# Fetching q, k and v of three batches head by head through GpSimd's queue, with a register for the head and a cast in flight

## The chip, the cores and the metric

The kernel runs on one core of a Trainium2 chip. The metric is the time of one run in device microseconds (us). The kernel before takes 238.6 us as the median of its runs (238.37 to 239.58). Every kernel that is compared below was run on one chip beside the kernel before, in the same rounds. A run in which the time lies over 1.5% above the fastest of its kernel is put down as slow. Ratios leave such runs out; the medians quoted are of all runs, and e10, e12 and e13 each have one slow run among them. The experiments ran in sets on different chips, on which the kernel before took 238.6 to 240.0 us, so kernels of different sets are compared best by their ratios.

The engines carry these names in the profile: PE is TensorE (matmuls), PEld its weight loads, DVE VectorE, ACT ScalarE, POOL GpSimd, SP SyncE, which here only issues DMA transfers.

## The reference

Attention with two kinds of heads is followed by a small feed-forward layer. Shapes: batch 4, 8 heads, sequence 768, head size 64; then 3,072 tokens of width 512 through a hidden layer of 2,048.

```python
scores = scale * np.matmul(q, k.transpose(0, 1, 3, 2))
causal = rel >= 0                                   # rel = query position - key position
stream_keep = causal & (is_sink | in_win)           # the first 4 keys, or the last 64
mask = np.where(retr[0, :, 0, 0, None, None], full_mask, stream_mask)   # by head
a = softmax of np.where(mask, scores, -1e9)
attn = np.matmul(a, v)
x = attn.transpose(0, 2, 1, 3).reshape(B * S, H * D)
h = x @ w_in
return (h - np.tanh(h)) @ w_out
```

Which heads see all earlier keys ("retrieval" heads) and which see only a window is known from the input `is_retrieval` at run time alone.

## The kernel before

The 3,072 tokens are worked in 12 tiles of 256 (three tiles a batch). The first batch (tiles 0 to 2) treats all heads alike and masks them. For batches 1 to 3 (tiles 3 to 11) the heads are put in the order of a rank, retrieval heads first, so that window heads can skip most scores. The rank is computed on the chip, and eight registers of GpSimd hold which head has which rank.

The program is made by a small planner. Every instruction is handed to it with an estimated duration in ns, its reads and writes and, for a transfer, its packets. It simulates the engines and writes each engine's instructions down in the order in which they ran in that simulation. Each engine then runs in that order on the chip.

```python
def op(self, eng, ns, fn, r=(), w=(), dma=None, prio=None, port=False, after=None, behind=None):
    ...   # dependencies from the keys in r and w; dma = (packets, ns of one packet)
```

For tiles 3 to 11 SP fetches fp32 q, k and v, each as two loads of 128 rows x 8 heads (1,024 packets of 256 bytes), and GpSimd casts to fp16, one rank at a time, the register choosing the head:

```python
op(
    "SP", max(420, 128 * nh * 1.1),
    lambda ...: nc.sync.dma_start(
        out=raw_of(nm, t)[:, i, h0 : h0 + nh, :],
        in_=src[b, h0 : h0 + nh, s0 : s0 + 128, :].rearrange("h p d -> p h d"),
    ), ..., dma=(128 * nh, 18.3), after=after,
)
...
def cast_ranked(t):
    for half in range(2):
        for nm in ("qk", "v"):
            for rank in range(half * HH, half * HH + HH):
                def fn(nm=nm, rank=rank):
                    at = bass.ds(regs["POOL"][rank], 1)
                    ...   # v in the same way
                    nc.gpsimd.tensor_copy(
                        out=t16[t % 2][:, :, :, rank : rank + 1, :],
                        in_=raws["rqk", t][0]()[:, :, :, at, :],
                    )
                op("POOL", 300 if nm == "v" else 430, fn, ...)
    for i in range(NB):          # two transposes by DMA on SP's queue, when all of q and k are cast
        nc.sync.dma_start_transpose(out=qk[b % 2][:, :, g * NB + i, 0:128], in_=t16[t % 2][:, i]...)
    ...
```

The transposed `qk` is what the score matmuls on TensorE read. So a tile goes: load, cast, transpose, scores. Tiles 1 and 2 already come by GpSimd's own queue with a cast in flight (`load_cast`, 1,024 packets an issue, no register), and so do the weights of the hidden and output layers.

The softmax here doesn't subtract the row's maximum and nothing guards it: scores larger than these inputs give would overflow.

Of the kernel before, what the change touches and what calls it, by code (L numbers as in the profile page):

```python
# [7 lines left out]
FP32 = mybir.dt.float32  # L8
# [8 lines left out]
class Plan:  # L17
# [16 lines left out]
    def op(self, eng, ns, fn, r=(), w=(), dma=None, prio=None, port=False, after=None, behind=None):  # L34
        i = len(self.ops)
        deps = set() if after is None else {after}
        for k in r:
            if k in self.writer:
                deps.add(self.writer[k])
            if k[0] in self.PSUM:  # L40
                deps.update(j for j in self.readers.get(k, ()) if self.ops[j][0] != eng)
            self.readers.setdefault(k, []).append(i)
# [16 lines left out]
    def run(self):  # L59
# [45 lines left out]
        while len(order) < n:  # L105
# [28 lines left out]
            _, ns, _, _, dma, _, port, _ = self.ops[i]  # L134
            self.start[i] = t
# [4 lines left out]
            for u in followers[i]:  # L140
                ready[u] = max(ready[u], t + ns)
                left[u] -= 1
                if not left[u]:
                    enqueue(u)
            if dma:
                packets, each = dma
                rings["POOL" if e == "POOL" else "SP"].append(
                    [i, t + ns + (1200 if e == "POOL" else 300), each, packets * each / 16]
                )
            else:  # L150
                finish(i, t + ns + self.RESULT[e])
# [6 lines left out]
def kernel(  # L158
# [35 lines left out]
    RAW, PT, XB, GB, XTB, THB, OB = 2, 3, 3, 3, 3, 3, 3  # L194
# [28 lines left out]
    gate = const.tile([1, 1], FP16, name="gate")  # L223
# [33 lines left out]
    def program(first):  # L257
# [30 lines left out]
        def paired(nm, t):  # L288

            return nm != "v" and t == 0  # L290

        def load(t, names="qkv", halves=(None,), blocks=range(NB), after=None):

            b, g = divmod(t, NG)
            for half in halves:
                h0, nh = (0, H) if half is None else (half * HH, HH)
                for nm in names:
                    src = {"q": q, "k": k, "v": v}[nm]
                    tag = "rv" if nm == "v" else "rqk"
                    if (tag, t) not in raws:  # L300
                        idx = rot[tag] = rot.get(tag, -1) + 1
                        shape = [128, NB, H, D] if nm == "v" else [128, NB, 2, H, D]
                        raws[tag, t] = (
                            lazy(raw_pool, shape, FP32, tag, f"raw_{tag}{t}"), idx
                        )
                    if paired(nm, t):
                        op(
                            "SP", max(420, 128 * nh * 1.1),
                            lambda nm=nm, src=src, h0=h0, nh=nh: nc.sync.dma_start(
                                out=raw_pairs(nm, t)[:, h0 : h0 + nh, :, :].rearrange(  # L310
                                    "p h e d -> p h (e d)"
                                ),
                                in_=src[b, h0 : h0 + nh, g * TT : (g + 1) * TT, :].rearrange(
                                    "h (p e) d -> p h (e d)", e=NB
                                ),
                            ),
                            w=[
                                key for x in (range(2) if half is None else (half,))
                                for key in raw_keys(nm, t, x)
                            ],  # L320
                            dma=(128 * nh, 26.0), after=after,
                        )
                        continue
                    for i in blocks:
                        s0 = g * TT + i * 128
                        op(
                            "SP", max(420, 128 * nh * 1.1),
                            lambda nm=nm, i=i, src=src, s0=s0, h0=h0, nh=nh: nc.sync.dma_start(
                                out=raw_of(nm, t)[:, i, h0 : h0 + nh, :],
                                in_=src[b, h0 : h0 + nh, s0 : s0 + 128, :].rearrange("h p d -> p h d"),  # L330
                            ),
                            w=[
                                key for x in (range(2) if half is None else (half,))
                                for key in raw_keys(nm, t, x, (i,))
                            ],
                            dma=(128 * nh, 18.3), after=after,
                        )
# [13 lines left out]
        def raw_keys(nm, t, half, blocks=range(NB)):  # L351
            tag = "rv" if nm == "v" else "rqk"
            return [(tag, raws[tag, t][1], nm, half, i) for i in blocks]
# [11 lines left out]
        def load_cast(t, w_after=(), names="qkv"):  # L365

            b, g = divmod(t, NG)
            for nm in names:
# [13 lines left out]
                if nm == "v":  # L382
                    for i in range(NB):
# [3 lines left out]
                            dma=(128 * H, 18.5),  # L387
                        )
                    continue
                for i in range(NB):  # L390
                    behind(
                        930, lambda fn=fn, i=i: fn((i,)), r=w_after,
                        w=[key for half in range(2) for key in t16_keys(nm, t, half, (i,))],
                        dma=(128 * H, 18.5),
# [37 lines left out]
        for half in range(2):  # L432
            load(0, "qk", (half,))
            load(0, "v", (half,))
# [102 lines left out]
        def by_rank(after):  # L537

            def dve(ns, fn, r, w):
                op("DVE", ns, fn, r=r, w=w, after=after)  # L540
# [82 lines left out]
                r=["A4", "A40", "A41", "A43"], w=["mS"], port=True, after=after,  # L623
# [4 lines left out]
                r=["mS3"], w=["mS"], port=True, after=after,  # L628
            )
            for e, et in (("POOL", Engine.Pool), ("DVE", Engine.DVE)):  # L630
# [7 lines left out]
                op(e, 900, get, r=["perm"], w=["regs" + e])  # L638
# [9 lines left out]
        def t16_keys(nm, t, half, blocks=range(NB)):  # L648
            return [("t16", t % 2, nm, half, i) for i in blocks]

        def cast_qk(t, engines, halves=range(2)):

            for half in halves:
                for nm, es in zip("qk", engines):
                    hs = slice(half * HH, half * HH + HH)
                    cast_op(
                        es[half], NB * HH * D,
                        lambda nm=nm, hs=hs: t16[t % 2][:, :, "qk".index(nm), hs, :],
                        lambda nm=nm, hs=hs: raw_of(nm, t)[:, :, hs, :],
                        r=raw_keys(nm, t, half), w=t16_keys(nm, t, half),  # L660
                    )

        def cast_ranked(t):
# [4 lines left out]
            for half in range(2):  # L668
                for nm in ("qk", "v"):
                    for rank in range(half * HH, half * HH + HH):  # L670

                        def fn(nm=nm, rank=rank):
                            at = bass.ds(regs["POOL"][rank], 1)
                            if nm == "v":
                                nc.gpsimd.tensor_copy(  # L675
                                    out=v1s[b]()[:, lo : lo + NB, rank : rank + 1, 0:D],
                                    in_=raw_of("v", t)[:, :, at, :],
                                )
                            else:
                                nc.gpsimd.tensor_copy(  # L680
                                    out=t16[t % 2][:, :, :, rank : rank + 1, :],
                                    in_=raws["rqk", t][0]()[:, :, :, at, :],
                                )

                        op(
                            "POOL", 300 if nm == "v" else 430, fn,
                            r=["regsPOOL"] + [
                                key for x in range(2) for n_ in nm for key in raw_keys(n_, t, x)
                            ],
                            w=[("v1", b, g, half)] if nm == "v" else [  # L690
                                key for n_ in nm for key in t16_keys(n_, t, half)
                            ],
                            port=True,
                        )
            for i in range(NB):

                def turn(i=i):
# [7 lines left out]
                    r=[key for half in range(2) for n_ in "qk" for key in t16_keys(n_, t, half)],  # L705
# [83 lines left out]
        def cast_v(t, engines=("POOL", "POOL"), halves=range(2)):  # L789
# [5 lines left out]
            for half in halves:  # L795
# [4 lines left out]
                    r=raw_keys("v", t, half), w=[("v1", b, g, half)],  # L800
# [27 lines left out]
        def st_T(n, eq="DVE", ek="DVE"):  # L828
            t, hp = divmod(n, HP)
            b, g = divmod(t, NG)  # L830
            for x, (nm, e) in enumerate((("q", eq), ("k", ek))):
# [9 lines left out]
                def turn(x=x, tp=tp):  # L841
# [7 lines left out]
                    "PE", 112, turn, r=t16_keys(nm, t, hp * 2 // HP) + ["ident"], w=[key],  # L849
# [412 lines left out]
        cast_qk(0, (("ACT", "ACT"), ("ACT", "DVE")), (0,))  # L1262
        load_cast(1, [("rv", 0, "v", 0, 1)], "qk")
# [10 lines left out]
        cast_v(0, ("POOL", "POOL"), (0,))  # L1274
        cast_qk(0, (("ACT", "ACT"), ("ACT", "DVE")), (1,))
# [8 lines left out]
        cast_v(0, ("POOL", "POOL"), (1,))  # L1284
# [16 lines left out]
        else:  # L1301
            load(2)
            scale_v(0, "POOL")
        scale_v(1)
        if first:

            def wait_tile_2():
                nc.sync.dma_start(out=gate[:], in_=t16[0][0:1, 0, 1, 0, 0:1])

# [133 lines left out]
```

## Time and profile before

| | before |
|---|---|
| median time | 238.6 us |
| profiled span | 236.7 us |
| TensorE busy | 221.5 us (94%) |
| GpSimd busy | 90.5 us (38%) |
| packets of SP's queue / of GpSimd's | 92,642 / 15,168 |
| granted TensorE clock, mean | 1.000 |

Two lines of the page show the row of 40 slices of the span (5.9 us each; a digit is the busy share in tenths) for GpSimd, and the clock that TensorE was granted.

```profile
POOL 5999420089818068480814904606300000000000
PEclk9999999999999999999999999999999999999999
```

GpSimd has whole slices with nothing to do, even between 40 and 160 us where it handles tiles 3 to 11, and the clock is full throughout. This is the timeline of GpSimd for part of a tile (start, length, then what ran; in brackets idle time before it and what ended it).

```profile
69.86 2.58 POOL L680 CAST t<-raw_rqk 128x256 f16 x6 [5.52 <-DMA raw_rqk<-in_k_dram]
...
74.51 2.13 POOL L675 CAST v<-raw_rv 128x128 f16 x6
```

Six casts of q and k take 2.58 us.

### The profile page before, as it was taken

How to read it: one execution, taken by the hardware profiler on the slowest of the kernel's cores; microseconds unless marked ns; L12 is line 12 of the kernel's file. 1: busy time of each engine (PE TensorE's matmuls, PEld its weight loads, DVE VectorE, ACT ScalarE, POOL GpSimd, SP SyncE). 2: the span in 40 equal slices, each digit the busy share in tenths (PEclk: the TensorE clock that was granted, in tenths of full speed). 3: DMA queues.
4: the chain of work that ended last, by engine and by line, in shares of the span. 5: the costliest groups of instructions: out<-in, count | busy, mean ns of one | idle time of the engine just before them, and what ended most of it. 6: DMA issues, size and time to landing. Idle time of an engine off the chain costs nothing. (4 is left out here: it accounts for less than half of the span.)

```text
span 236.7 us, 5895 instructions
## 1 busy us (share of the span) xinstructions
PE 221.5 (94%) x2220; PEld 157.8 (67%) x2220; DVE 139.0 (59%) x343; ACT 143.6 (61%) x221; POOL 90.5 (38%) x218
## 2 busy tenths in 40 slices
PE   0889899999999999999999999999999999999991
PEld 0346687756776777777676777776776777777661
DVE  1856665864488657767666655667766546443300
ACT  3668677884588387466686649537759464444320
POOL 5999420089818068480814904606300000000000
PEclk9999999999999999999999999999999999999999
DMA  5999999999997999979989695998712101310121
GB/s 128 209 140 172 204 181 204 197 228 224 206 225 182 151 248 184 227 153 206 239 168 214 136 186 130 186 171 179 134 47 66 38 31 47 90 38 9 44 89 51
DMA packets 108130, 35.29 MB, mean 149 GB/s; under 512 B 100290, under 2 KB 104642, under 8 KB 108098
## 3 DMA queue, kind: packets, MB, share of 16 engines
q1 hardware_dynamic: 92642, 28.98, 60.5%
q0 software_dynamic: 15168, 5.77, 20.7%
q8 instruction: 18, 0.29, 0.5%
q10 hardware_dynamic: 288, 0.14, 0.2%
q14 instruction: 14, 0.11, 0.2%
HBM read 27.27 MB, written 6.29 MB: 142 GB/s over the span
## 5 line engine op out<-in xcount | busy, mean ns | idle before, releaser
L1135 PE MATMUL ph<-xT,win 128*128 128x256 f16 x768 | 101.7, 273 | 0.6 <-DMA win<-in_moe_w_in_dram 0.3
L1194 PE MATMUL po<-wout,gt 128*128 128x512 f16 (+1 forms) x400 | 98.0, 371 | 0.3 <-ACT ot L1170 0.3
L1148 ACT ACTIVATE th<-ph 128x512 f32<-128x512 f32 x96 | 57.6, 601 | 59.6 <-PE ph L1135 58.2
L1155 DVE SCALAR_TENSOR_TENSOR gt<-th,ph 128x512 f16<-128x512 f32 x96 | 65.4, 684 | 44.9 <-ACT th L1148 44.4
L1135 PEld LDWEIGHTS <-win 128*128 128x128 f16 x768 | 80.0, 114 | 13.0 <-issue 1.9
L961 ACT ACTIVATE pt<-sc 128x1024 f16<-128x1024 f32 (+1 forms) x78 | 68.5, 926 | 11.4 <-PE sc L941 10.9
L1194 PEld LDWEIGHTS <-gt 128*128 128x128 f16 x400 | 36.4, 98 | 24.6 <-issue 0.9
L680 POOL CAST t<-raw_rqk 128x256 f16 x72 | 28.5, 440 | 63.3 <-DMA raw_rqk<-in_k_dram 48.1
L1030 PEld LDWEIGHTS <-pt 128*128 128x128 f16 x552 | 25.9, 98 | 10.4 <-issue 0.9
L1030 PE MATMUL av<-v,pt 128*128 128x65 f16 x304 | 26.0, 195 | 0.1
L941 PE MATMUL sc<-qk 64*128 64x128 f16 (+1 forms) x412 | 23.8, 240 | 1.7 <-DVE qk L826 1.7
L941 PEld LDWEIGHTS <-qk 64*128 64x128 f16 x412 | 13.7, 94 | 13.5 <-issue 8.9
L675 POOL CAST v<-raw_rv 128x128 f16 x72 | 21.1, 335 | 4.2 <-DMA raw_rv<-in_v_dram 4.2
L1060 DVE TENSOR_TENSOR x16t<-av,rinv 128x128 f32 x72 | 20.8, 289 | 2.3 <-DVE rinv L1050 0.3
L1030 PE MATMUL av<-vf,pt 128*128 128x65 f16 x248 | 19.6, 193 | 0.0
L1170 ACT ACTIVATE ot<-po 128x512 f32<-128x512 f32 (+1 forms) x24 | 14.3, 596 | 8.5 <-PE po L1194 8.4
L996 DVE TENSOR_TENSOR pt<-pt,m 128x1024 f16<-128x1024 f16 x16 | 12.3, 768 | 8.0 <-ACT pt L961 8.0
L1050 DVE RECIPROCAL rinv<-av 128x4 f32<-128x4 f32 x48 | 8.6, 179 | 13.4 <-PE av L1030 13.4
L986 DVE TENSOR_TENSOR pt<-pt,mS 128x512 f16<-128x512 f16 x24 | 9.8, 449 | 6.7 <-ACT pt L961 6.7
L843 PEld LDWEIGHTS <-t 128*128 128x128 f16 x48 | 3.9, 107 | 8.9 <-ACT t L644 6.8
L523 DVE TENSOR_SCALAR m<-A,thr 128x512 f16<-128x512 f16 x16 | 7.4, 501 | 1.7 <-PE sc L928 1.2
L751 POOL TENSOR_TENSOR vf<-v,rflagr 128x260 f16<-128x260 f16 x12 | 7.5, 634 | 0.0
(95 smaller groups left out, 90.8 us busy)
## 6 DMA issues: line engine op xcount, KB each, us to landing
out_dram<-ot SPq DMA_DIRECT2D x23, 256.0 KB, 2.3
raw_rqk<-in_q_dram SPq DMA_DIRECT2D x20, 256.0 KB, 4.7
raw_rqk<-in_k_dram SPq DMA_DIRECT2D x20, 256.0 KB, 4.5
raw_rv<-in_v_dram SPq DMA_DIRECT2D x18, 256.0 KB, 4.4
win<-in_moe_w_in_dram POOLq DMA_DIRECT2D x4, 512.0 KB, 8.8
wout<-in_moe_w_out_dram POOLq DMA_DIRECT2D x4, 512.0 KB, 12.4
raw_rv<-in_v_dram SPq DMA_DIRECT2D x4, 128.0 KB, 4.7
t<-in_q_dram POOLq DMA_DIRECT2D x4, 128.0 KB, 9.5
```

Source lines behind the costliest of these rows:

```text
L675: nc.gpsimd.tensor_copy(out=v1s[b]()[:, lo : lo + NB, rank : rank + 1, 0:D], in_=raw_of("v", t)[:, :, at, :],)
L680: nc.gpsimd.tensor_copy(out=t16[t % 2][:, :, :, rank : rank + 1, :], in_=raws["rqk", t][0]()[:, :, :, at, :],)
L941: nc.tensor.matmul(out=sc()[:, hh, o : o + nb * 128].rearrange("p (i c) -> p i c", c=128), lhsT=ks.rearrange("p i c -> p (i c)")[p_, jb * ...
L961: lambda pt=pt, gi=gi, wid=wid, sc=sc: nc.scalar.activation(out=pt()[:, :, 512 * gi : 512 * gi + wid], in_=sc()[:, :, 0:wid], func=AF.Exp, ...
L996: nc.vector.tensor_mul(out=pv, in0=pv, in1=m4[:, h0 : h0 + 2, 256:512].unsqueeze(2).to_broadcast([128, 2, 2, 256]),)
L1030: nc.tensor.matmul(out=av()[:, i, hh, :], lhsT=pt()[:, hh, co : co + 128], rhs=vv, start=(jb == first_jb), stop=(jb == qb),)
L1060: nc.vector.tensor_mul(out=x16s[t]()[:, :, at, :], in0=av()[:, :, hh : hh + 1, 0:D], in1=rinv()[:, :, hh : hh + 1].unsqueeze(3).to_broadca ...
L1135: nc.tensor.matmul(out=ph()[:, j, :], lhsT=w()[:, cb, c0 + fb % 4 : c0 + 512 : 4], rhs=xTs[t]()[:, cb, :], start=(cb == 0), stop=(cb == HP ...
L1148: lambda: nc.scalar.activation(out=th()[:], in_=ph()[:], func=AF.Tanh, scale=1.0 / XS),
L1155: lambda: nc.vector.scalar_tensor_tensor(out=gts[t]()[:, u * FU : (u + 1) * FU, :], in0=th()[:], scalar=-XS, in1=ph()[:], op0=ALU.mult, op ...
L1170: nc.scalar.activation(out=ot()[:, c0:c1], in_=po()[:, c0:c1], func=AF.Copy, scale=1.0 / XS)
L1194: nc.tensor.matmul(out=po()[:, c0:c1], lhsT=gts[t]()[:, f, ts * 128 : ts * 128 + 128], rhs=w_out_t[f // 4]()[:, f % 4, c0:c1], start=(f == ...
```

## The change

The intent is to have no fp32 copies and no casts for batches 1 to 3. GpSimd fetches each head's 256 rows straight to its rank's place, the head's number taken from the register, and the DMA casts on the way.

```diff
-    RAW, PT, XB, GB, XTB, THB, OB = 2, 3, 3, 3, 3, 3, 3
+    RAW, PT, XB, GB, XTB, THB, OB = 1, 4, 3, 3, 3, 3, 3
...
-        def cast_ranked(t):
+        def load_ranked(t, names):
...
+            for nm in names:
+                for rank in range(H):
+                    def fn(nm=nm, src=src, rank=rank):
+                        at = bass.ds(regs["POOL"][rank], 1)
+                        o = (
+                            v1s[b]()[:, lo : lo + NB, rank, 0:D] if nm == "v"
+                            else t16[t % 2][:, :, "qk".index(nm), rank, :]
                         )
+                        nc.gpsimd.dma_start(
+                            out=o,
+                            in_=src[b, at, g * TT : (g + 1) * TT, :].rearrange(
+                                "h (i p) d -> p i (h d)", p=128
+                            ),
+                        )
+                    behind(
+                        380, fn, r=["regsPOOL"], ...
+                        dma=(NB * 128, 14.0), after=PACE.get((t, nm)),
+                    )
...
+        def turn_ranked(t):        # the two transposes, as before
...
-        for half in range(2):
-            load(0, "qk", (half,))
-            load(0, "v", (half,))
+        for names, pairs in [("qk", (0,)), ("qk", (1,)), ("v", (0, 1)), ("qk", (2, 3)), ("v", (2, 3))]:
+            load(0, names, pairs)
```

Each of the nine tiles thus has 24 issues of 256 packets (3 tensors x 8 heads) in place of 6 issues by SP and 16 casts. Besides, q and k of tile 0 come by pairs of heads, the rank computation comes a tile earlier, one more buffer holds softmax results (`PT`), and some of the planner's constants change.

## The prediction

> **What bounds the kernel now.** I read the page's busy table and its row of slices, then stretches of the span with each engine's busy time, then TensorE's waits, then the queues, the groups and single transfers.
>
> ```profile
> PE 221.5 (94%) x2220; PEld 157.8 (67%) x2220; DVE 139.0 (59%) x343; ACT 143.6 (61%) x221; POOL 90.5 (38%) x218
> PE   0889899999999999999999999999999999999991
> ```
> TensorE (PE) is busy for 221.5 of 236.7 us, so all that a change can win without less matmul work is the other 15.2 us. The stretches (columns: length, then busy us of PE, weight loads, VectorE, ScalarE, GpSimd) say where these lie.
>
> ```profile
> 0.00:14.00 14.00, 7.12 (x46) 3.17 (x46) 7.08 (x21) 7.34 (x12) 10.86 (x26) 1.00 1.18 156
> 14.00:40.00 26.00, 23.48 (x276) 17.88 (x273) 16.35 (x41) 19.13 (x34) 13.75 (x17) 1.00 1.46 186
> 40.00:80.00 40.00, 39.05 (x446) 27.35 (x445) 26.83 (x82) 27.51 (x41) 22.31 (x59) 1.00 1.04 207
> 80.00:220.00 140.00, 140.00 (x1381) 101.53 (x1380) 86.06 (x196) 86.21 (x130) 43.60 (x117) 1.00 0.68 137
> 220.00:236.70 16.70, 11.81 (x81) 7.86 (x79) 2.63 (x5) 3.37 (x6) 0.00 (x0) 1.00 0.15 52
> ```
> Idle TensorE: 6.9 us before 14, 2.5 from 14 to 40, 1.0 from 40 to 80, **nothing from 80 to 220**, 4.9 in the tail. A busy TensorE need not be a full one, so I counted the stretch from 200 to 220 us: 93 matmuls of 256 columns and 46 of 512, at the 0.107 and 0.213 us that back-to-back starts in the timeline show, make 9.9 + 9.8 = 19.7 of 20 us. It is full. The granted clock is 1.00 throughout. The longest TensorE waits are the first one and very little else:
>
> ```profile
> PE tp0q L843 <- ACT t L644: 6.0, 1, 6.0
> PE sc L941 <- DVE qk L826: 1.7, 3, 0.7
> PE tp0k L843 <- ACT t L644: 0.5, 1, 0.5
> ```
> The casts that the change removes, GpSimd's two big groups, do wait for transfers, but nobody on TensorE waits long for them (one 0.4 us wait of a weight load). So they are off the path.
>
> ```profile
> L680 POOL CAST t<-raw_rqk 128x256 f16 x72 | 28.5, 440 | 63.3 <-DMA raw_rqk<-in_k_dram 48.1
> L675 POOL CAST v<-raw_rv 128x128 f16 x72 | 21.1, 335 | 4.2 <-DMA raw_rv<-in_v_dram 4.2
> ```
>
> **What the Trainium skill says.** "DMA: Bandwidth & Descriptors", section "Rules for kernel authors", has it that casting in flight is for a DMA issued from GpSimd; this kernel already does so for batch 0's tiles 1 and 2, and it works. The same page, "Issuing engines are not separate DMA queues": all queues end on the same 16 engines, so changing the ring adds no bandwidth. The trace agrees: the two queues below share one busy row of DMA that is at nine tenths through most of the first 145 us. "SBUF — State Buffer", section "SBUF: two separate sides", warns that VectorE in a two-port mode locks GpSimd out of writing descriptors. The trace shows little of it: the four q issues of 1,024 descriptors took 0.89 to 1.10 us while VectorE was making masks.
>
> ```profile
> q1 hardware_dynamic: 92642, 28.98, 60.5%
> q0 software_dynamic: 15168, 5.77, 20.7%
> L378 POOL DMA_DIRECT2D t<-in_q_dram x4: 887/933/1098, 6.1 to 19.4; - x4
> L415 POOL DMA_DIRECT2D wout<-in_moe_w_out_dram x4: 543/566/616, 18.0 to 32.5; - x4
> ```
>
> **The change part by part.**
> *Removed*: 144 casts on GpSimd, 28.5 + 21.1 = 49.6 us; 54 loads by the SP ring. *Added*: 9 tiles x 24 = 216 GpSimd loads of one head and 256 packets. What one issue costs is read from two rows: 0.57 us for wout (few, long rows) and 0.93 us for 1,024 packets. One of 256 short packets should lie at or below the lower of these, if a fixed part and a part per packet make up the rest; I take 0.5 us, with 0.4 to 0.62 as limits. 216 x 0.5 = 108 us, so GpSimd goes from 90.5 to 90.5 - 49.6 + 108 = about 149 us (63%), 127 at 0.4 and 175 at 0.62. **GpSimd gets busier, not freer.** Per tile it is 24 x 0.5 = 12 us plus about 3 us of vf copies (0.6 x 2 + 1.0 + 0.4 and a little), 15 us, against a tile's period of (231.8 - 18.9)/12 = 17.7 us from the first hidden-layer matmul to the last output one. It fits; at 0.62 us, 14.9 + 3 = 17.9, it just does not.
>
> *Packets*: one load in the old trace is 1,024 packets and 16 more (q0: 12 casts x 1,024 + 4 x 512 + 4 x 128 + 20 x 16 = 15,168, exactly). So q1 loses 54 x 1,040 = 56,160 and falls to about 36,500; q0 gains 216 x 272 = 58,752 and becomes about 73,900. Bytes counted fall by 54 x 0.131 = 7.1 MB, to about 28 MB, as fp16 is written. DMA gets lighter, but it is not the bound after 40 us, so this wins nothing by itself.
>
> *Shared port*: VectorE has 41% free and is not the bound; its faster masks win nothing either.
>
> *The beginning* also changes: q and k of tile 0 come by pairs of heads, and VectorE takes one cast. Now the first q transfer (512 packets) ends when ScalarE's cast starts, 5.33, and the tiny flags transfer ended by 4.46; so the data add 0.87 us. Half the data is about 0.43 us less, and a cast of 256 instead of 512 columns some 0.2 us less than 0.62: the first transpose at about 5.3, not 6.0, a gain of 0.7 us. The wait for k (0.5 us) mostly goes too, as does part of what follows: 1.0 to 1.5 us in all, if something to do follows.
>
> *Moves*: the instruction listing shows the same 2,220 matmuls on the run path in another order. Tile 2's first transposes come after 56 hidden-layer matmuls instead of 64, tile 3's first scores after 128 hidden and 28 output ones instead of 160 and 48: there the data are needed earlier. Tile 2 comes through the same saturated ring as before; its k landed at 33.98 us at the latest, when SP's gate on it let go. By TensorE's old clock the new place is at about 32.8, less the gain at the start 31.7: a new wait of up to 2 us, which gives the start's gain back. For tile 3, 24 loads follow the last wout issue (32.5 us); the listing lets each wait for the eighth load before it. From 33 us, with wout landing 10 to 13 us after issue, I get the last k issued near 45 and landed near 47, and 3.7 us of transposing: 50.5. TensorE wants it at about 50.2 on the old clock. A wait of 0 to 1.5 us.
>
> **Sum**: start -1.3; less of the scattered 3.5 us of waits between 14 and 80, -1.0; tile 2's wait +0.7, tile 3's +0.5; from 80 us on 0. That is -1.1 us of 238.7: **237.6 us**.
>
> **The rivals.**
> 1. *GpSimd becomes the bound.* Its in-order stream of loads at 0.62 us or more, with register arithmetic, and each waiting for an eighth one before, delivers a tile in 18 to 20 us instead of 17.7. Nine tiles would lose 3 to 10 us, partly bought off by the lead of a tile: 240 to 246 us. For it: GpSimd's 149 us estimate is steep, and one load now serves one head. Against it: the loads have 157 us (33 to 190), and the old issues were hardly slowed by VectorE.
> 2. *The whole gain is hidden.* The ring brings tile 2 at the same 34 us, TensorE waits there for what it had won, and from there both kernels are equal: 238.5 to 239.5. For it: a saturated ring in 17 to 36 us; against it: work that TensorE can do beside.
> 3. *DMA relief matters more than I think.* Lighter loads bring weights and tile 2 earlier, and nearly all of the 3.5 us and 1.5 us of the start go: 234.5. Beyond that the full stretch from 80 to 220 us stops it; over 2% (below 233.9) would need 4.8 of 9.4 idle us before 40.
>
> **Range and chances.** Centre 237.6; I give the first rival some 10%, the third's extreme 5%. Runs of before spread over 1.2 us. So 235.2 to 240.8, faster 0.05, same 0.85, slower 0.10.
>
> **What would show it.** TensorE's first matmul at about 5.3 us; TensorE busy about 221 us and full from 80 to 220; no casts by rank, GpSimd at 127 to 175 us; q0 near 73,900 and q1 near 36,500 packets; a wait of a TensorE transpose of tile 2 (tp) for t by DMA around 32 us, and perhaps one of the first ranked scores for qk around 50 us. Wrong would be: TensorE idle in every tile after 60 us behind qk or v (the first rival), an issue far over 0.62 us, or idle before 40 us falling below 6 us (the third).

## The result, and the profile after

The changed kernel is correct and takes **294.1 us** (median of four runs, 292.94 to 296.57), against 238.6 us. The ratio is 1.233, with a 95% interval of 1.224 to 1.242. Ratios here are the mean time of one kernel's fast runs over that of the other's fast runs of the same rounds, so they are not quite the ratios of the medians quoted. The prediction of 237.6 us was wrong, far outside its range.

The page of the changed kernel: busy times, then rows of the span in 40 slices of 7.3 us.

```profile
PE 235.1 (81%) x2220; PEld 163.5 (56%) x2220; DVE 138.3 (47%) x344; ACT 143.7 (49%) x222; POOL 197.1 (68%) x291
...
PE   3877999599194299798089999399579999999993
...
POOL 6993749799989599699799489799789600000000
PEclk9999999969879589999559999979959999999998
```

TensorE runs the same 2,220 matmuls, but it is idle for 291.2 - 235.1 = 56.1 us instead of 15.2, which is 40.9 us more. It is also busy for 13.6 us more than the 221.5 us of before. Together that is the span's whole 54.5 us. GpSimd went from 90.5 to 197.1 us and is busy for 121.1 of the 140 us from 80 to 220, where it had empty slices before. The stretches of the span (columns as in the prediction) set against those of before:

```profile
0.00:14.00 14.00, 7.91 (x54) 3.66 (x56) 7.05 (x25) 7.35 (x14) 11.11 (x27) 1.00 1.11 161
14.00:40.00 26.00, 22.04 (x266) 16.65 (x264) 19.23 (x58) 18.95 (x33) 17.79 (x23) 1.00 1.49 195
40.00:80.00 40.00, 30.56 (x327) 21.33 (x326) 18.55 (x47) 19.94 (x31) 36.33 (x53) 0.88 0.92 92
80.00:220.00 140.00, 108.81 (x1003) 74.81 (x1002) 61.95 (x149) 63.86 (x94) 121.11 (x175) 0.86 0.83 90
```

Up to 40 us little has changed. From 80 to 220 us TensorE, which was full, issues 1,003 matmuls instead of 1,381, and its clock averages 0.86. What it waits for, the two largest of TensorE's waits (total us, times, longest us), was not there before:

```profile
PE sc L942 <- DMA qk<-t: 21.4, 6, 9.4
PE ph L1136 <- DMA xT<-x16t: 19.8, 3, 9.4
```

The first is the score matmuls waiting for the transposed q and k. The second is the hidden layer waiting for the attention result of such a tile, transposed in its turn. One tile's chain can be followed on GpSimd, SP and TensorE in three timelines. First GpSimd:

```profile
43.34 5.75 POOL L676 DMA_DIRECT2D t<-in_k_dram  x8
49.03 5.79 POOL L676 DMA_DIRECT2D v<-in_v_dram  x8
...
65.54 5.76 POOL L676 DMA_DIRECT2D t<-in_k_dram  x8
```

Eight issues take 5.75 us, so **one issue takes 0.72 us**, and they stand end to end. (The records of single issues are a little longer, as each overlaps the next.) The last of the k loads of the second tile shown is issued by 65.54 + 5.76 = 71.3 us. Then SP and TensorE:

```profile
73.39 2.63 SPq L698 DMA_TRANSPOSE qk<-t  x2
```

```profile
79.11 0.93 PE L942 MATMUL sc<-qk 64*128 64x256 f16 x10 [6.27 <-DMA qk<-t]
```

SP issues the two transposes at 73.4 us, when the last k has landed (SP's wait before this line is for k), and TensorE, after 6.3 us of idling, begins the scores at 79.1 us. The stretches of 3 us around this wait show what it costs beyond itself.

```profile
72.00:75.00 3.00, 0.85 (x4) 0.20 (x2) 0.85 (x2) 0.60 (x1) 3.00 (x6) 1.00 0.82 67
75.00:78.00 3.00, 0.00 (x0) 0.10 (x1) 0.00 (x0) 0.00 (x0) 3.00 (x5) 0.91 1.45 167
78.00:81.00 3.00, 1.89 (x15) 1.25 (x15) 0.18 (x1) 1.24 (x2) 3.00 (x5) 0.50 1.57 241
81.00:84.00 3.00, 3.00 (x12) 1.47 (x10) 1.31 (x2) 1.08 (x2) 2.90 (x5) 0.50 0.80 50
84.00:87.00 3.00, 3.00 (x43) 2.06 (x41) 1.39 (x6) 2.20 (x3) 1.77 (x3) 0.95 0.13 8
```

The figure behind the five busy times is the granted clock. It falls to 0.50 once TensorE has been idle, and stays there for some 5 us after work has come back. The timeline of TensorE shows it on equal work, eight hidden-layer matmuls ahead of the wait and eight behind it:

```profile
70.95 1.03 PE L1136 MATMUL ph<-xT,win 128*128 128x256 f16 x8
...
79.98 1.89 PE L1136 MATMUL ph<-xT,win 128*128 128x256 f16 x8
```

Such stretches account for the 13.6 us of longer busy time: the same matmuls run on a clock that is halved after a long wait. A mean clock of 0.914 means some 50 of the 291.2 us at 0.50. By the trace TensorE was busy for about 30 of them, which at full clock would have been some 15 us shorter, by an estimate. The Trainium skill states this, in "TensorE: Matmul & The Clock Gate", section "HAM oscillation — how this bites in real kernels": a wait for DMA that is long enough makes the clock gate throttle again, and the next work starts cold. The trace agrees, with 1.03 us becoming 1.89 behind an idle time of 6.3 us.

### The profile page after: what moved, and what is told of

Read it like the earlier page. It is cut to its first block, busy times and chain, and to the rows that moved or that the text cites. A ratio compares the mean times of both kernels' runs of the same rounds, so it can differ in the third digit from the quotient of the medians.

```text
span 291.2 us, 6241 instructions
## 1 busy us (share of the span) xinstructions
PE 235.1 (81%) x2220; PEld 163.5 (56%) x2220; DVE 138.3 (47%) x344; ACT 143.7 (49%) x222; POOL 197.1 (68%) x291
## 2 busy tenths in 40 slices
DMA packets 110755, 28.25 MB, mean 97 GB/s; under 512 B 102912, under 2 KB 107264, under 8 KB 110720
## 3 DMA queue, kind: packets, MB, share of 16 engines
q0 software_dynamic: 73920, 12.86, 55.4%
q1 hardware_dynamic: 36512, 14.82, 22.7%
## 5 line engine op out<-in xcount | busy, mean ns | idle before, releaser
L1136 PE MATMUL ph<-xT,win 128*128 128x256 f16 x768 | 107.2, 282 | 20.2 <-DMA xT<-x16t 19.8
L1195 PE MATMUL po<-wout,gt 128*128 128x512 f16 (+1 forms) x400 | 103.7, 385 | 0.0
L1136 PEld LDWEIGHTS <-win 128*128 128x128 f16 x768 | 81.6, 116 | 37.4 <-DMA xT<-x16t 20.2
L676 POOL DMA_DIRECT2D t<-in_q_dram x72 | 52.1, 755 | 5.7 <-DMA wout<-in_moe_w_out_dram 2.6
L676 POOL DMA_DIRECT2D v<-in_v_dram x72 | 52.4, 831 | 0.0
L676 POOL DMA_DIRECT2D t<-in_k_dram x72 | 52.0, 781 | 0.0
L942 PE MATMUL sc<-qk 64*128 64x128 f16 (+1 forms) x412 | 26.0, 257 | 22.5 <-DMA qk<-t 21.4
L942 PEld LDWEIGHTS <-qk 64*128 64x128 f16 x412 | 15.4, 101 | 36.1 <-issue 19.0
L1031 PE MATMUL av<-v,pt 128*128 128x65 f16 x304 | 27.7, 201 | 0.0
L1031 PE MATMUL av<-vf,pt 128*128 128x65 f16 x248 | 21.2, 200 | 0.0
L771 POOL COPY vf<-v 64x260 f16<-64x260 f16 (+1 forms) x9 | 4.5, 496 | 16.0 <-DMA v<-in_v_dram 15.8
```

What stands on the lines that cost most here:

```text
L676: nc.gpsimd.dma_start(out=o, in_=src[b, at, g * TT : (g + 1) * TT, :].rearrange("h (i p) d -> p i (h d)", p=128),)
L942: nc.tensor.matmul(out=sc()[:, hh, o : o + nb * 128].rearrange("p (i c) -> p i c", c=128), lhsT=ks.rearrange("p i c -> p (i c)")[p_, jb * ...
L1031: nc.tensor.matmul(out=av()[:, i, hh, :], lhsT=pt()[:, hh, co : co + 128], rhs=vv, start=(jb == first_jb), stop=(jb == qb),)
L1136: nc.tensor.matmul(out=ph()[:, j, :], lhsT=w()[:, cb, c0 + fb % 4 : c0 + 512 : 4], rhs=xTs[t]()[:, cb, :], start=(cb == 0), stop=(cb == HP ...
L1195: nc.tensor.matmul(out=po()[:, c0:c1], lhsT=gts[t]()[:, f, ts * 128 : ts * 128 + 128], rhs=w_out_t[f // 4]()[:, f % 4, c0:c1], start=(f == ...
```

## The experiments

Fourteen kernels were run. The diffs are against the changed kernel. The expectations use letters for the theories. **A** says that GpSimd's in-order stream of issues sets the end, in the variants A1 (because of the register) and A2 (because of a fixed time of each issue). **D** says that the wrong 380 ns that the planner is told for one issue does. **E** says that an issue costs by its packets, and **F** that the loads lack fp16 buffers. Where other letters occur, the expectation itself says what they stand for.

### e1_static: no register

```diff
-                        at = bass.ds(regs["POOL"][rank], 1)
+                        at = slice(rank, rank + 1)
```

This is wrong: the heads are no longer put by rank.

> The changed kernel with a constant head number in place of the register in each of the 216 loads (wrong result on purpose: heads are not reordered). Theory A1, the register makes an issue dear: an issue falls from 0.72 us to 0.4 to 0.5 us (the old rows gave 0.57 us for few packets and 0.93 us for 1,024), GpSimd busy falls to about 140 us, time to 238 to 245 us. Rival A2, any load of one head with its 256 packets costs about 0.7 us: issue stays at 0.70 to 0.78 us, time stays at 285 to 296 us.

It took 296.2 us, 1.240 times the time of before [1.232, 1.248]. This is the k row of the line of the issues (duration in ns: least, median, most), in the changed kernel and then in this run.

```profile
L676 POOL DMA_DIRECT2D t<-in_k_dram x72: 721/784/822, 43.3 to 223.9; - x72
```

```profile
L676 POOL DMA_DIRECT2D t<-in_k_dram x72: 716/723/793, 42.9 to 225.3; - x72
```

An issue without the register takes 0.72 us as well. The median record is shorter by 0.06 us, but the issues stand 0.72 us apart in both kernels. So the register costs nothing that shows in the pace, and the time belongs to the issue, as A2 had it.

### e2_whole: few large issues with the same cast

```diff
-                        if ranked(t + 2):
-                            load_ranked(t + 2, names)
-                        elif names:
+                        if names:
```

Tiles 3 to 11 come as tile 2 does, in 6 issues of 1,024 packets, without ranks (wrong). The cast is the same as in the changed kernel, the packets are nearly the same (71,328 in GpSimd's queue for 73,920), and the issues are a quarter.

> The changed kernel with tiles 3 to 11 loaded and cast in flight as tiles 1 and 2 are, six loads of 1,024 packets a tile with all eight heads and no register (wrong result on purpose). The same bytes and nearly the same packets on the same ring, 54 issues instead of 216. Theory A, the number of issues on GpSimd is what costs: 54 x 0.9 = 49 us of issuing, time 236 to 239 us. Rival B, casting in flight through GpSimd's ring itself is slow (transfers, its completion, or contention of the two rings): time stays above 270 us.

It took 251.1 us, 1.0475 [1.040, 1.056]. GpSimd's busy time fell to 90.0 us. Neither range was met. With the 216 issues, 43 of the 55.5 us of loss go. But the planner's wrong 380 ns go with them, since these larger issues are planned with 930 ns and take 0.88; e4_plan separates the two. And 12 us of loss remain in a kernel whose GpSimd is idle for most of the time.

### e3_oldload: the rest of the change without its main part

The start by pairs, the earlier ranks, the buffers and the planner's constants stay; tiles 3 to 11 are fetched by SP and cast by rank as before (`cast_ranked` put back, `RAW` 2). The result is correct.

> The changed kernel, but tiles 3 to 11 come as in the kernel before: fp32 copies by SP, casts by rank on GpSimd; the new start, the new places of by-rank work, four pt buffers and the new planner stay. Correct result. Theory A: 236.5 to 239 us, as the loss is all in the ranked loads. Rival C, the new order or the new start costs: clearly above 240 us.

It took 239.9 us, 1.003 [0.997, 1.008], the same as before. The rest of the change is neither the cause nor a gain. This gives the later experiments their base.

### e4_plan: the planner told 800 ns

```diff
-                        380, fn, r=["regsPOOL"],
+                        800, fn, r=["regsPOOL"],
```

Same instructions on every engine, in another order. The result is correct.

> The changed kernel with the planner told 800 ns for a ranked issue instead of 380 ns; the same instructions in another order. Theory A, GpSimd's stream of issues is the bound: its 216 issues still take 156 us and more, time 280 to 294 us. Rival D, the plan was only misled by 380 ns and TensorE waits in a bad order: time falls below 260 us.

It took 261.65 us, 1.0955 [1.088, 1.103]. Neither expectation was met, as both theories are partly true. Some 32.5 us of the 55.5 came from an order that was laid out for loads twice as fast as the chip's: TensorE's idle time fell from 56.1 to 260.6 - 227.2 = 33.4 us and its busy time from 235.1 to 227.2 us, with the same loads. What is left over goes with a GpSimd that has no time to spare, as the stretches of e4_plan show. That no other order would do better is not shown.

```profile
120.00:160.00 40.00, 37.25 (x328) 25.64 (x326) 20.74 (x50) 19.71 (x30) 39.55 (x58) 1.00 0.92 104
160.00:200.00 40.00, 37.49 (x370) 27.88 (x370) 23.61 (x54) 23.84 (x36) 39.45 (x58) 1.00 1.06 125
```

GpSimd is busy for 39.5 of 40 us. It is full, and TensorE, with 37.4, is not.

### e5_vbatch: fewer issues, ranks kept

On top of e4_plan, v of a head is fetched once for all three tiles of a batch (768 packets), 168 issues instead of 216. The result is correct.

```diff
+                if nm == "v" and g:
+                    continue
+                n_t = NG if nm == "v" else 1
...
-                            v1s[b]()[:, lo : lo + NB, rank, 0:D] if nm == "v"
+                            v1s[b]()[:, lo : lo + n_t * NB, rank, 0:D] if nm == "v"
```

> The re-planned kernel (261.7 us) with v fetched once for a whole batch by head: 24 issues of 768 packets in place of 72 of 256, so 168 issues in place of 216. Correct result. Theory A, the rest of the loss after re-planning is GpSimd's stream of issues at 0.72 us: 144 x 0.72 + 24 x 0.85 = 124 us in place of 156, GpSimd per tile 14 + 3 = 17 us against TensorE's 17.7, so time falls to 238 to 246 us. Rival B, transfers and their landing bound: the packets are the same, so time stays at 256 to 264 us.

It took 248.6 us, 1.037 [1.032, 1.042]: 13 us less than e4_plan (14 by the ratios) for 33 us less of GpSimd's time (165.3 instead of 198.4). It lies between the two ranges, and meets neither. The count of issues matters; that something else holds once GpSimd has some slack is a guess here.

### e6_merged: fewer still

q and k too are fetched for up to three tiles of a batch in one issue of 256, 512 or 768 packets, 96 issues in all, into fp16 tiles of a whole batch (`PT` 3, the planner told 730, 780 and 850 ns). The result is correct.

```diff
+        RUNS = {3: 1, 4: 2, 6: 3, 9: 3}
...
-                        380, fn, r=["regsPOOL"],
+                        {1: 730, 2: 780, 3: 850}[n_t], fn, r=["regsPOOL"],
```

> By head, a register's head number, cast in flight, but one load spans up to three tiles: tile 3 alone, tiles 4 and 5 together, batches 2 and 3 whole: 96 issues (24 of 256, 24 of 512, 48 of 768 packets), and the planner told 730, 780 and 850 ns. Correct result. pt has three buffers again for room. Theory A: issues of 0.72, 0.76 and 0.83 us sum to 75 us, GpSimd is no bound, time 236 to 242 us. Rival B, the in-flight path is slow by its packets: above 250 us. Rival E, an issue costs by packets: an issue of 768 packets takes over 1.5 us.

It took 254.8 us, 1.062 [1.055, 1.068], more than e5_vbatch. A's 236 to 242 us were missed, and B's range of above 250 us was met. It still measures the issue. In its timeline of GpSimd, the first line has issues of 256 packets, the second of 768:

```profile
44.68 5.74 POOL L684 DMA_DIRECT2D t<-in_k_dram  x8
...
84.26 6.63 POOL L684 DMA_DIRECT2D t<-in_q_dram  x8
```

Eight take 5.74 us at 256 packets and 6.63 us at 768, which is 0.72 and 0.83 us each, and the 1,024 of e2_whole stand 0.88 us apart. A line through these is about **0.65 us fixed plus 0.06 us for every 256 packets**. Below 256 it does not hold for every transfer: the output layer's weights, 128 packets an issue, took 0.57 us. Theory E is false: a quarter of the packets does not cost a quarter. With GpSimd at 117.0 us the kernel is 15 us slower than before nevertheless, so A is not all of it.

### e7_extra: more of GpSimd's time

On top of e4_plan, behind each of the 216 loads GpSimd writes a small scratch tile. The result is correct.

```diff
+                    behind(204, lambda: nc.gpsimd.memset(scratch[:], 1.0), w=["scratch"])
```

> The re-planned kernel (261.7 us) with one more GpSimd memset of 0.2 us behind each of the 216 ranked loads; correct result. Theory A, GpSimd's stream is the bound: span up by about 216 x 0.2 = 43 us, less what slack it has, 285 to 310 us. Rival B, transfers or order bound: GpSimd has 24% idle, 261 to 268 us.

It took 294.5 us, 1.228 [1.218, 1.238], 32.8 us more than e4_plan (31.6 by the ratios); GpSimd's busy time grew by 31.8 us, to 230.2. The distance from one load to the next went from 0.72 to 0.855 us in the timeline, and 216 x 0.135 = 29 us. Nearly every microsecond that is put on GpSimd comes out at the end: in e4_plan GpSimd is the bound, shown by adding to it. (The planner was told of the memsets, and laid out a new order here too.)

### e8_wholeplan and e9_wholedeep: is e2's remainder the plan, or the buffers?

e8 is e2_whole with the planner told 25 ns a packet for tiles 3 to 11 instead of 15. e9 is e8 with four fp16 tiles for q and k instead of two (both wrong, as e2).

```diff
-                            dma=(128 * H, 15.0), after=after,
+                            dma=(128 * H, 15.0 if t < NG else 25.0), after=after,
...
-    t16 = [const.tile([128, NB, 2, H, D], FP16, name=f"t16_{x}") for x in range(2)]
+    t16 = [const.tile([128, NB, 2, H, D], FP16, name=f"t16_{x}") for x in range(4)]
```

> The unordered fetch of eight heads a load (251.1 us, wrong result on purpose) with the planner told that a packet of tiles 3 to 11 takes 25 ns in place of 15. Same instructions in another order. If those 12.5 us over the kernel before are a bad order, as the planner reckoned loads too fast, time falls to 237 to 243 us. If the in-flight path itself costs, it stays at 248 to 252 us.

> The unordered fetch of eight heads a load with the planner's 25 ns (252.8 us, wrong result on purpose), and four fp16 buffers for q and k in place of two. That kernel's GpSimd waited 18.7 us to load until transposes had read a buffer. Theory F (the fp32 copies were also buffers, and taking them away makes the loads wait): time falls to 239 to 246 us. Theory G (transfers cast in flight occupy the 16 engines longer, 34 against 22 ns a packet by the queues' shares, and slow the transposes beside them): stays at 249 to 254 us.

They took 252.8 us, 1.055 [1.049, 1.061], and 252.1 us, 1.056 [1.047, 1.065]. e8 lies just above its second range, e9 within that of G. Neither a plan with longer packets nor more buffers wins e2_whole's loss back.

### e11_vbatchdeep and e12_plandeep: buffers again, with ranks

Four fp16 tiles on top of e5_vbatch and of e4_plan, both correct; the edit is e9's second.

> e5_vbatch (248.6 us, correct result, 168 issues) with four fp16 buffers for q and k. Theory F: 240 to 245 us. Theory A alone (issue rate): GpSimd still has 124 us of issues, 246 to 250 us.

> The re-planned kernel (261.7 us, correct result, 216 issues) with four fp16 buffers for q and k. Theory A (216 issues of 0.72 us bind): 257 to 263 us. Theory F: below 252 us.

They took 248.3 us, 1.039 [1.032, 1.045], and 260.6 us, 1.091 [1.084, 1.098], against 248.6 and 261.65 us with two. F is false.

### e10_fp32pool: SP's old loads on GpSimd's queue

e3_oldload, with one thing changed: the 54 fp32 loads of tiles 3 to 11 are issued by GpSimd instead of SP. No cast in flight, the same bytes, and the casts by rank stay. The result is correct.

```diff
+                    eng = "POOL" if first and fast and t >= NG else "SP"
...
+                    if eng == "POOL":
+                        behind(930, fetch, **kw)
+                    else:
+                        op("SP", max(420, 128 * nh * 1.1), fetch, **kw)
```

> As e3_oldload (239.9 us: fp32 copies, casts by rank), but GpSimd instead of SP issues the 54 loads of tiles 3 to 11, without a cast in flight. Correct result. It separates the ring and its in-order issue from the cast in flight. Theory H (loads on GpSimd wait behind its own copies, and that is the 12 us that few loads still cost): 247 to 253 us, GpSimd busy about 90 + 49 = 139 us. Theory G or F: 238 to 243 us.

It took 255.7 us, 1.064 [1.052, 1.076], where e3_oldload took 239.9. By the ratios that is (1.064 - 1.003) x 238.6 = 14.6 us: for the queue alone, or for the time it takes of GpSimd (137.8 us busy, after 89.7), or for the order that GpSimd imposes. It lies above H's range, and G and F are missed. The two runs after it separate time and order.

### e13_busypool: GpSimd's time without its queue

e3_oldload with SP's loads kept; where e10 has an issue, GpSimd runs a memset of the same length. The result is correct.

```diff
+                    op("SP", max(420, 128 * nh * 1.1), fetch, **kw)
+                    if busy:
+                        behind(930, lambda: nc.gpsimd.memset(scratch[:], 1.0), w=["scratch"], after=after)
```

> As e3_oldload (SP issues the 54 fp32 loads, 239.9 us), with a GpSimd memset of some 0.9 us at each place where e10_fp32pool (255.7 us) has GpSimd issue a load. Correct result. GpSimd's added time is that of e10, but loads keep their own ring and sequencer. If e10's loss is GpSimd's time taken from its casts and vf copies: 250 to 257 us. If it is that loads wait in GpSimd's order and go out through its ring: 238 to 243 us.

The line of the memsets shows that they took what an issue takes.

```profile
L346 POOL MEMSET scratch<- x54: 921/931/1026, 33.6 to 158.9; 128x1000 f16 x54
```

It took 238.0 us, 0.994 [0.985, 1.002], with GpSimd at 137.4 us, the same as before. GpSimd's lost time is not what e10 pays.

### e14_sporder: GpSimd's order without its queue

e13_busypool, and in addition each of SP's loads waits for a one-element memset by GpSimd in its destination, so that the loads go out when GpSimd gets to them, but by SP's queue. The result is correct.

```diff
+                        behind(
+                            100, lambda nm=nm, i=i: nc.gpsimd.memset(raw_of(nm, t)[:, i, 0, 0:1], 0.0),
+                            w=raw_keys(nm, t, pairs, (i,)), after=after,
+                        )
```

> As e13_busypool (238.0 us), and each SP load of tiles 3 to 11 must also wait for a one-element GpSimd memset of its destination, at the place where e10_fp32pool (255.7 us) has GpSimd issue that load. So the loads follow GpSimd's order but keep SP's hardware ring. Correct result. If the order behind GpSimd's other work is what e10 pays for: 248 to 256 us. If GpSimd's ring (its transfers, beside SP's transposes) is: 238 to 243 us. A slow result is the less clear of the two, as SP's transposes can then wait behind a load.

It took 239.4 us, 1.002 [1.000, 1.005]. GpSimd's order is not it either. What remains is the queue through which the data go, and two things that change along with it. The first is the size of packets. This is GpSimd's queue (packets, MB, share of 16 engines) in e10, then in e13:

```profile
q0 software_dynamic: 19488, 19.93, 45.3%
```

```profile
q0 software_dynamic: 15168, 5.77, 20.4%
```

The 54 loads bring 4,320 packets, 80 each, where SP's queue needed 1,040 packets for the same load: without a cast, GpSimd's queue moves these rows in packets of 4,096 bytes by the trace, and SP's in packets of 256. The second is the planner's order. It models the two queues apart, and the traces show another order on TensorE in each of e3, e10, e13 and e14; the three of these that load by SP's queue all take 238 to 240 us, but whether a better order would help e10 was not tried.

The stretch of 40 to 160 us of e10, then of e13:

```profile
40.00:160.00 120.00, 110.56 (x1159) 78.05 (x1158) 70.52 (x164) 72.86 (x108) 94.87 (x191) 0.97 0.92 178
```

```profile
40.00:160.00 120.00, 119.17 (x1261) 85.68 (x1260) 76.64 (x183) 78.05 (x117) 104.44 (x215) 1.00 0.95 194
```

With the same bytes by the same 16 DMA engines, TensorE gets through 1,159 matmuls by GpSimd's queue and 1,261 by SP's. The lists of transfers (size, where it is given, then median us from issue to landing) say what was slower. This is e10:

```profile
raw_rqk<-in_q_dram POOLq DMA_DIRECT2D x18, 256.0 KB, 7.0
...
qk<-t SPq DMA_TRANSPOSE x18, 5.8
```

And this is e13, with the loads on SP's queue:

```profile
raw_rqk<-in_q_dram SPq DMA_DIRECT2D x19, 256.0 KB, 4.3
...
qk<-t SPq DMA_TRANSPOSE x18, 3.7
```

The loads of q land after 7.0 us instead of 4.3 (k after 5.5 instead of 4.9, v after 6.5 instead of 4.7), and the transposes, which are SP's in both, after 5.8 instead of 3.7: both of the links that make a tile ready are longer.

## Why the prediction was wrong

**The step that failed is the cost of an issue.** The prediction took 0.5 us with limits of 0.4 and 0.62. The trace has 0.72: the 72 issues of q are busy for 52.1 us, those of k for 52.0. So the room that the prediction saw in each tile was not there, nor was its "0" from 80 us on. The reasoning was that 256 short packets should cost no more than the lower of two old rows, the 0.57 us of the output layer's weights. But that row has another shape of transfer, and the row that has this one's shape, 0.93 us for 1,024 packets, was read as mainly a price per packet. e6_merged and e2_whole show it to be mainly fixed, about 0.65 us. The old trace had a third row that the prediction left out, that of the hidden layer's weights:

```profile
L401 POOL DMA_DIRECT2D win<-in_moe_w_in_dram x4: 757/760/770, 11.1 to 17.3; - x4
```

That is 0.76 us for 512 packets. A line through it and the 0.93 us of 1,024 gives an estimate of 0.67 us at 256, above the prediction's upper limit. With 0.72 the prediction's own formula for a tile gives 24 x 0.72 + 3 = 20.3 us against a period of 17.7, and so 9 x 2.6 = 23 us of loss. The measured pace is (230.3 - 33.7) / 9 = 21.8 us a tile, from the first issue to the last one's end; GpSimd also stood idle for 22.4 us in all before its copies of v (`vf`), until v had landed. GpSimd's 149 us, with 175 as its upper limit, was 197.1.

**Rival 1 came true, and was too small too.** It named the mechanism, GpSimd's stream behind which TensorE waits in every tile, gave it 10%, and said 240 to 246 us. The waits at the scores, e4_plan's full GpSimd and the 32.8 us of e7_extra show the mechanism. Three things were missing from its sum:

- *The plan.* The prediction read the order of instructions as given and never asked what it was built on. 380 ns were told, and 0.72 us came. TensorE then met the scores of each tile too early (its two largest waits), and GpSimd its copies of v (22.4 us of idling, some 7 in e4_plan). This costs 294.1 - 261.65 = 32.5 us (e4_plan), the largest part.
- *The queue.* Without the pressure on GpSimd's time, loads through its queue still cost 11 to 16 us (e2, e8 and e9; e10 against e3, with e13 and e14 to exclude GpSimd's time and order). The prediction held that changing the ring adds no bandwidth, and put no cost on it.
- *The clock.* TensorE's idle time was not thought to make its busy time longer. It did by 13.6 us, which is contained in the parts above and not added to them.

These parts do not simply add up: 32.5 us for the plan, some 11 for the issues' number (e4_plan against e2_whole, 261.65 - 251.1) and some 11 for the queue (e2_whole against e3_oldload, 251.1 - 239.9) is the path of one sequence of edits, in which the later bounds hide behind the earlier ones.

**"DMA gets lighter" was right in bytes and wrong in time.** Packets came out as worked out (q0 73,920 for 73,900, q1 36,512 for 36,500; 28.25 MB for 28). But a packet of the new kind kept its engine busy for longer, by an estimate from the queues' shares. q0's part went from 20.7% of 236.7 us to 55.4% of 291.2 us; this is (161.3 - 49.0) x 16 / 58,752 packets = 30.6 ns each. The fp32 packets that SP's queue lost were (143.2 - 66.1) x 16 / 56,160 = 22.0 ns each. Half the bytes written took more of the engines' time. GpSimd's queue alone does not make this: without a cast, and in packets of 4,096 bytes, e10's loads come to (114.8 - 48.4) x 16 / 55,296 = 19.2 ns for every 256 bytes, by the shares of e10 and e3. That the engines' time decided anything is not shown. These shares of the queues carry it:

```profile
q0 software_dynamic: 73920, 12.86, 55.4%
q1 hardware_dynamic: 36512, 14.82, 22.7%
```

**The beginning was right at first and lost again.** TensorE's first matmul came 1.4 us earlier than before, at 4.6 us (predicted 5.3), and by 40 us nothing was left of it: 29.95 us of TensorE work after (7.91 + 22.04) against 30.60 before. This is rival 2, as long as one looks at the start alone, and e3_oldload, which has the same start and no other burden, confirms that it is worth nothing: 239.9 us.

**Tile 3** was expected to have its last k issued at 45 us and its scores at 50.5. The trace has the last k issue ending at 49.1 us and the first transpose at 51.0; the first score matmuls that waited for one began at 58.0, after 3.2 us of idling where up to 1.5 had been expected. A wait of tile 2's transposes, up to 2 us, is not among TensorE's waits at all.

**What stays open.** Why transfers by GpSimd's queue land later and slow SP's transposes beside them was not separated. e10 shows it with fp32 loads in packets of 4,096 bytes, e2 with cast ones in small packets, so the two need not have one cause; whether it is the size of packets, the way in which the DMA engines alternate between queues, or an order that was laid out for other landing times, no run tells. In e2, e6, e8, e9 and e10 the end of the kernel, from VectorE's last operation on, also takes 6.6 to 7.6 us instead of 4.5 to 4.8 in the kernels before and after and in e3, e4 and e5. So 2 to 3 us of what is put down to the queue fall after the last computation; no run explains that. And why e6_merged with 96 issues is slower than e5_vbatch with 168 was not pursued; its `PT` of 3 and its planner's time of a packet differ too. No version beat the kernel before: e13_busypool's 238.0 us lies within the interval of the same time.

## What to carry to other kernels

When loads are moved to GpSimd, count issues, not bytes: each held GpSimd for 0.72 us with 256 packets and 0.88 with 1,024, and the count per tile times that must stay well under the tile's period. A planner's constant that was never measured is part of the change: put the measured duration in and look at the order again before judging the idea. And a queue that is free (here SP's) should keep loads that feed the critical path, since the same loads by GpSimd's queue went with a kernel slower by some 15 us, though the size of their packets and the planner's order changed with them.

## What the Trainium skill lacked or had wrong

- "DMA: Bandwidth & Descriptors", section "Anatomy of one DMA — SWDGE (gpsimd) path", gives the generation of descriptors as "small, variable", and says that many can be emitted before the cost shows. The small slope agrees (about 0.06 us for 256 packets), but the page lacks the fixed time for which GpSimd is held by each issue: 0.72 us at 256 packets, 0.83 at 768, 0.88 at 1,024 in these runs, with or without a register in the address (713 ns is the shortest of the loads by head).
- The same page, section "Issuing engines are not separate DMA queues", says that issuing from several engines only saves the sequencer's time. By itself this does not foretell what was measured: the same 54 fp32 loads took the kernel to 255.7 us from GpSimd's queue and 239.9 us from SP's, with SP's transposes landing after 5.8 instead of 3.3 us, and neither GpSimd's time (238.0) nor its order (239.4) explains it. The packets' size, 4,096 bytes for 256, and the planner's order were not separated from the queue.
- No page that was read gives the price of a cast in flight in the DMA engines' time: here an estimated 30.6 ns for a 256-byte fp32 packet cast on its way, against 22.0 ns for the fp32 packet copied by SP's queue and 19.2 ns for 256 bytes by GpSimd's queue without a cast, in packets of 4,096 (e10).
